# One score unit in sixty-four moved from ScalarE's exponential to a copy by VectorE and a power on GpSimd

## The chip, the cores and the metric

The kernel runs on one core of a Trainium2 chip. Its engines work side by side, each through its own instructions in order, and wait for each other by semaphores: TensorE (PE in the profile) multiplies matrices into eight PSUM banks, ScalarE (ACT) computes exponentials, VectorE (DVE) does elementwise work, copies and transpositions, GpSimd (POOL) so far only makes a few constants, and SyncE's queue (SP) starts transfers. The metric is the device time of one execution in microseconds.

## The reference

Two attentions over the same input `x` (2048 positions, width 640, 32 heads of 20) are mixed by a gate per position. The first is full softmax attention, the second a sliding one over 8 positions 2 apart.

```python
g = _sigmoid((x * gate_w).sum(-1, keepdims=True))
a = _A_ref(x, A_wqkv, A_wo)          # softmax(q k^T / sqrt(20)) v, all 2048 keys, then wo
b = _B_ref(x, B_wqkv, B_wo)          # the same over pos, pos-2, ..., pos-14
return g * a + (1 - g) * b
```

## The kernel before

Full attention is cut into 32 groups: 4 blocks of 512 queries (`qc`) times 8 quads of heads (`q`). A group has 64 units, 16 blocks of 128 keys (`kb`) times the 4 heads of the quad (`j`). For a unit, PE computes 128 keys by 512 queries of scores into one PSUM bank (L956), ACT takes the exponential into SBUF (`ebuf`, L969), and PE multiplies that by V and adds to the group's result in bank 5 (L977; V has a column of ones, so the sum of the exponentials comes with it). Units are taken in steps of three and two in turn, in banks 0 to 2 and 3 to 4; one ACT instruction serves a whole step. The scores of step s + 2 are issued right behind the exponential of step s. The four heads of a quad lie on different rows of the PE array for the scores and on different columns for the product.

At the end of a group `do_norm` transposes bank 5 into `rg` (L586) and `gen_norm` divides by the sums (L594, L595, L600) and transposes back into one of `NOT` = 16 slots of `oTn` (L603). The first product of the next group overwrites bank 5, so it waits for L586.

All other work is threaded between these steps by a planner written in Python, which keeps a clock for each engine, advanced by costs that are written at each operation. Work is cut into lanes (generators): `gen_k`, `gen_q` and `gen_v` project k, q and v for the coming groups; `gen_F` and `gen_K` make the sliding attention of a block of 512 positions, the former mainly projections and products, the latter mainly pairs of VectorE operations (L853 and L857, with L847 and L863 at the ends of a block of 128); `gen_fold` multiplies finished blocks with the output weights and stores them; `gen_prefold` does most of that for the last block, with copies at L653, and `last_fold` the rest (L665, L672) behind the loop. Lanes share PSUM banks 6 and 7: `take` claims one, `give` frees it when VectorE has copied it out. A lane has a first and a last step, counted by `gstep(g) = int(g * KBN * 4 / 2.5)`, 25.6 steps to a group, and is served when it is behind its share and the planner's clock has room. What has not been done when its result is needed is forced on the spot; what is left at the end of the loop is forced there, ahead of `last_fold`. The order that results is fixed: on the chip each engine runs its list as it stands.

The weights for a group's q projection are put in place by a VectorE copy within SBUF (L360); the projection (L378) waits for it. It is copied out at L537, made absolute at L538, corrected by a matmul at L543 that subtracts a bound of the scores, and copied to `qT` at L545.

Of the kernel before, what the change touches and what calls it, by code (L numbers as in the profile page):

```python
# [5 lines left out]
FP32 = mybir.dt.float32  # L6
# [212 lines left out]
def _build(ctx, nc, A_x, A_wqkv, A_wo, B_wqkv, B_wo, gate_w, out):  # L219
# [48 lines left out]
    qabs = sb([P, 512], BF16, "qabs")  # L268
    NEB = 3
    ebuf = [sb([P, 1536], BF16, "ebuf%d" % i) for i in range(NEB)]  # L270
    rg = [sb([P, 512], FP32, "rg%d" % i) for i in range(2)]
    rr = [sb([P, 16], FP32, "rr%d" % i) for i in range(2)]
    rgn = [sb([P, 16, 32], BF16, "rgn%d" % i) for i in range(2)]
    NOT = 16
    oTn = sb([P, NOT, 512], BF16, "oTn")
    itmp = oTn[:, 13, 0:256].bitcast(I32)
    stmp = oTn[:, 14, 0:320].bitcast(I32).rearrange("p (c k) -> p c k", c=CN)
    stmpf = oTn[:, 15, 0:320].bitcast(FP32).rearrange("p (c k) -> p c k", c=CN)
    zg = sb([P, KBN], FP32, "zg")
    gA = sb([P, 4 * KBN], FP32, "gA")  # L280
    gB = sb([P, KBN], FP32, "gB")
# [21 lines left out]
    def fap(t, first, dims):  # L303
        return bass.AP(tensor=t, offset=first.offset, ap=[[first.ap[0][0], P]] + dims)
# [30 lines left out]

    T("pe", pe_warm, reads=["ident", ("rgn", 0)], writes=[("bk", 7)])
    T("dve", lambda e: e.memset(e0[:, :], 0.0), writes=["e0"])
    T("dve", lambda e: e.memset(nsel[:, :], 0.0), writes=["nsel"])
    for j in range(4):
        T("dve", lambda e, j=j: e.memset(e0[32 * j:32 * j + 1, :], 1.0), writes=["e0"])  # L340
# [84 lines left out]
    def give(b, evac):  # L425
        held[b] = False
        if cur[0] is not None:
            cur[0].hold -= 1
        free_at[b] = evac.fin + 80.0
# [92 lines left out]
    def gen_q(gi):  # L522
        qc, q = divmod(gi, NQUAD)
        i = gi % 2
        yield ("dve", 370.0, 0.0)
        yield after(mk_wq(q, i))
        while qc == 0 and not kl[q].done:
            yield ("poll",)
        b = yield from take()
        yield from chain(b, proj_mms(b, WqP[i], qc), [("WqP", i), "xT"])  # L530
        yield ("dve", 690.0, 0.0)
        yield after(q_abs(b))
        yield ("pe", MM, 1.0)
        give(b, q_fin(b, gi, q))

    def q_abs(b):
        T("dve", lambda e: e.tensor_copy(qtmp[:, :], bank[b]), reads=[("bk", b)], writes=["qtmp"], cost=690)  # L537
        return T("dve", lambda e: e.tensor_scalar(qabs[:, :].bitcast(I16), qtmp[:, :].bitcast(I16), 0x7FFF, None,  # L538
                                                  op0=ALU.bitwise_and),
                 reads=["qtmp"], writes=["qabs"], cost=300)  # L540

    def q_fin(b, gi, q):
        T("pe", lambda e: e.matmul(bank[b], KM[:, q, :], qabs[:, :], start=False, stop=True, skip_group_check=True),  # L543
          reads=["qabs", ("KM", q)], accum=[("bk", b)], cost=MM)
        return T("dve", lambda e: e.tensor_copy(qT[gi % NQT][:, :], bank[b]), reads=[("bk", b)],  # L545
                 writes=[("qT", gi % NQT)], cost=690)

# [36 lines left out]
    def do_norm(gi):  # L584
        i = gi % 2
        return T("dve", lambda e: e.transpose(rg[i][:, :], bank[OB]), reads=[("ob", j) for j in range(4)],  # L586
                 writes=[("rg", i)], cost=720)

    def gen_norm(gi):
        qc, q = divmod(gi, NQUAD)  # L590
        i = gi % 2
        sl = gi % NOT
        yield ("dve", 420.0, 0.0)
        T("dve", lambda e: e.reciprocal(rr[i][:, :], rg[i][:, 0:512:32]), reads=[("rg", i)], writes=[("rr", i)], cost=240)  # L594
        T("dve", lambda e: e.tensor_tensor(rr[i][:, :], rr[i][:, :], gA[:, 16 * qc:16 * qc + 16], ALU.mult),  # L595
          reads=["gA"], writes=[("rr", i)], cost=180)
        rg_v = fap(rg[i], rg[i][:, 1:2], [[32, 16], [1, DH]])
        rr_b = fap(rr[i], rr[i][:, 0:1], [[1, 16], [0, DH]])
        yield ("dve", 500.0, 0.0)
        T("dve", lambda e: e.tensor_tensor(rgn[i][:, :, 1:1 + DH], rg_v, rr_b, ALU.mult),  # L600
          reads=[("rg", i), ("rr", i)], writes=[("rgn", i)], cost=500)
        yield ("dve", 710.0, 0.0)
        T("dve", lambda e: e.transpose(oTn[:, sl, :], rgn[i][:, :, :]), reads=[("rgn", i)], writes=[("oTn", sl)], cost=710)  # L603
        normdone[gi] = True
# [330 lines left out]
    free_at[6] = free_at[7] = t_  # L935


    units = [(qc, q, kb, j) for qc in range(QCN) for q in range(NQUAD) for kb in range(KBN) for j in range(4)]
    steps = []
    u = 0  # L940
    while u < len(units):
# [24 lines left out]
    def mk_exp(s):  # L966
        b0 = ST[s % 2][0]
        n = len(steps[s])
        return T("act", lambda e: e.activation(ebuf[s % NEB][:, 0:512 * n], ps[:, b0 * 512:(b0 + n) * 512], ACTF.Exp, scale=SCALE),  # L969
                 reads=[("bk", b0 + i) for i in range(n)], writes=[("ebuf", s % NEB)], cost=ED[n])  # L970

    def mk_pv(s, us):

        def fn(e):
            ins = None
            for i, (qc, q, kb, j) in us:
                ins = e.matmul(bank[OB][32 * j:32 * j + DH + 1, :], vA[:, q, kb, VW * j:VW * j + DH + 1],  # L977
                               ebuf[s % NEB][:, i * 512:(i + 1) * 512], start=(kb == 0), stop=(kb == KBN - 1))
            return ins

        rd = {("ebuf", s % NEB)}
        wr, ac = [], []
        for i, (qc, q, kb, j) in us:
            rd.add(("vA", q, kb // 3))
            (wr if kb == 0 else ac).append(("ob", j))
        T("pe", fn, reads=sorted(rd, key=str), writes=wr, accum=ac, cost=320)
# [6 lines left out]
    def lane(gen, name, s0, s1, total, pos=None):  # L993
        g = _Lane(gen, name, s0, s1, total)
        if pos is None:
            lanes.append(g)
        else:
            lanes.insert(pos, g)
        return g
# [59 lines left out]
        return int(g * KBN * 4 / 2.5)  # L1059

    kl, vl, ql, foldl = {}, {}, {}, {}
    vl[0] = lane(gen_v(0, 2), "v0", 0, 18, 10)
    lane(gen_late(), "late", 22, gstep(3), 1)
    FWIN = ((1.0, 8.3), (8.3, 13.2), (13.3, 18.3), (18.4, 23.5))
# [14 lines left out]
    for s in range(NS):  # L1079
# [4 lines left out]
        if first:  # L1084
            ng = gi + 1
            if ng < QCN * NQUAD:
                nqc, nq_ = divmod(ng, NQUAD)
                g_end = gstep(gi + 1)
                if nqc == 0:
                    kl[nq_] = lane(gen_k(nq_), "k%d" % nq_, s, g_end - 7, 20.0, 0)  # L1090
                    if nq_ % 2 == 1 and nq_ < NQUAD - 1:
                        p = (nq_ + 1) // 2
                        vl[p] = lane(gen_v(p), "v%d" % p, s + 2, gstep(gi + 2) - 2, 16.0)
                    ql[ng] = lane(gen_q(ng), "q%d" % ng, s + 4, g_end - 4, 6.0, 1)
                else:
                    ql[ng] = lane(gen_q(ng), "q%d" % ng, s + 2, g_end - 5, 6.0, 0)
        E = mk_exp(s)
        if s + 2 < NS:
            nxt = steps[s + 2]
# [8 lines left out]
            mk_qk(s + 2)  # L1108
        n1 = len(steps[s + 1]) if s + 1 < NS else 1
        lim = E.fin + ED[n1]  # L1110
        near = s + 1 < NS and (steps[s + 1][-1][2], steps[s + 1][-1][3]) == (KBN - 1, 3) or (
            s + 1 < NS and steps[s + 1][0][0:2] != steps[s + 1][-1][0:2])
        lim_pe = lim + 250.0
        lim_dve = lim + (0.0 if near else 450.0)
# [2 lines left out]
        def flush(must):  # L1117
            while pend:
                s0, i0, un0 = pend[0]
                g0 = un0[0:2]  # L1120
                obk = sch.bufs[("ob", 0)]
                if un0[2] == 0 and not must and obk[1]:
                    if max(t.fin for t in obk[1]) > clk["pe"] + 100.0:
                        return
                part = []
                while pend and pend[0][0] == s0 and pend[0][2][0:2] == g0:
                    _, i1, un1 = pend.pop(0)
                    part.append((i1, un1))
                for (_, un1) in part:
                    key = (un1[1], un1[2] // 3)  # L1130
                    if key not in vdone:
                        late.append((s, "v") + key)
                        force(vl[un1[1] // 2], s, lambda key=key: key in vdone)
                mk_pv(s0, part)
                if part[-1][1][2] == KBN - 1 and part[-1][1][3] == 3:
                    g1 = g0[0] * NQUAD + g0[1]
                    if g1 == 0 and not vl[0].done:
                        late.append((s, "gate", 0))
                        force(vl[0], s)
                    if g1 >= NOT and not folddone.get((g1 - NOT) // NQUAD):  # L1140
                        fl = foldl[(g1 - NOT) // NQUAD]
                        late.append((s, "fold", fl.name))
                        force(fl, s)
                    do_norm(g1)
                    lane(gen_norm(g1), "norm%d" % g1, s, s + 1, 1.0, 0)
# [63 lines left out]
```

## Time and profile before

| what | us |
|---|---|
| median of 2 runs | 1102.41 (1098.44 and 1106.39) |
| span of the profiled execution, first to last instruction | 1091.2 |
| exponentials, 819 instructions, busy | 956.0 |
| scores L956 and products L977, busy | 372.9 and 373.8 |
| VectorE busy | 579.7 |
| GpSimd busy | 0.7 |
| first exponential, start | 27.8 |
| last transposition of bank 5 (L586), start | 1081.0 |

The profile gives no time of its own for the profiled execution besides its span; the median of the runs is 11.2 us above it, which holds what lies ahead of the first instruction and behind the last. A row of the profile names the line, the engine, the operation, the tile written and the tile read with their shapes, then how often, the busy time and the mean of one in ns, and the idle time of the engine just before with what ended it. The groups are 29.2 to 35.5 us apart, from one L586 to the next.

### The profile page before, as it was taken

To read this page: it belongs to the slowest core of one execution; us is meant where nothing else is said; L and a number is where in the kernel's file an instruction comes from. 1 tells how busy PE (TensorE), PEld (TensorE's weight loads), DVE (VectorE), ACT (ScalarE), POOL (GpSimd) and SP (SyncE) were. 2 spreads that over 40 slices of the span, in tenths; PEclk is the share of its full clock that TensorE was granted. 3 is DMA by queue.
4 is the path that set the end of the run, shared out by engine and by line. 5 is a ranking of instruction groups with operands and counts; after the bars stand their busy time and mean duration, and the time that the engine had idled before them with its cause. 6 is when DMAs were issued, how large, how long until landed. Compare 5 with 4: busy or idle time off the path is not lost.

```text
span 1091.2 us, 15504 instructions
## 1 busy us (share of the span) xinstructions
PE 969.2 (89%) x5820; PEld 289.7 (27%) x5894; DVE 579.7 (53%) x1055; ACT 971.4 (89%) x842; POOL 0.7 (0%) x6
## 2 busy tenths in 40 slices
PE   6978899998798898989998988998888899799997
PEld 3323333322222222123332122233222223222231
DVE  4355434443635755762467767225787723777512
ACT  4868889988999988989999989999998989898996
POOL 0000000000000000000000000000000000000000
PEclk9879989998999756689998677999976699755695
DMA  8000000000000000000000000000000000000000
GB/s 277 1 1 15 17 1 2 1 23 9 1 2 1 1 1 1 1 1 7 7 7 7 1 1 1 7 8 7 7 2 1 1 7 13 7 1 1 1 1 25
DMA packets 11356, 12.79 MB, mean 12 GB/s; under 512 B 2708, under 2 KB 10644, under 8 KB 11284
## 3 DMA queue, kind: packets, MB, share of 16 engines
q1 hardware_dynamic: 9028, 11.27, 3.2%
q8 instruction: 49, 0.80, 0.3%
q10 hardware_dynamic: 2256, 0.53, 0.2%
q14 instruction: 23, 0.19, 0.1%
HBM read 9.18 MB, written 2.62 MB: 11 GB/s over the span
## 4 chain that ended last, share of the span: by engine, by line
PE 63%; ACT 21%; issue 9%; DVE 6%; DMA 1%; ACTq 0%; SPq 0%; DVEq 0%
ACT ebuf L969 21%; PE ps L956 20%; PE ps L378 19%; PE ps L977 19%; PE ps L453 2%; PE ps L543 1%; DVE bw L853 1%; PE ps L722 1%; DMA x_tm<-in_A_x_dram 1%; DVE blkacc L857 1%; PE ps L823 1%; DVE rg L586 1%; DVE qT L545 1%; DVE qtmp L537 0%; DVE WvB L672 0%
## 5 line engine op out<-in xcount | busy, mean ns | idle before, releaser
L969 ACT ACTIVATE ebuf<-ps 128x1536 bf16<-128x1536 f32 (+1 forms) x819 | 956.0, 1245 | 84.9 <-PE ps L956 64.3
L956 PE MATMUL ps<-qT,kT 32*128 32x512 bf16 x2048 | 372.9, 448 | 87.7 <-ACT ebuf L969 69.8
L977 PE MATMUL ps<-ebuf,vA 128*21 128x512 bf16 x2048 | 373.8, 452 | 3.3 <-DVE rg L586 1.2
L956 PEld LDWEIGHTS ps<-qT,kT 32*128 32x128 bf16 x2048 | 87.3, 93 | 370.5 <-PE ps L956 153.2
L977 PEld LDWEIGHTS ps<-ebuf,vA 128*21 128x21 bf16 x2048 | 77.7, 90 | 239.3 <-issue 229.7
L853 DVE TENSOR_TENSOR bw<-vB,bw 128x640 f32<-128x640 bf16 x112 | 91.9, 820 | 2.2
L857 DVE TENSOR_TENSOR blkacc<-blkacc,bw 128x640 f32<-128x640 f32 x96 | 79.0, 823 | 2.8
L739 DVE TENSOR_TENSOR prod<-qk 128x512 bf16<-128x512 bf16 x160 | 57.7, 418 | 22.3 <-PE ps L722 22.1
L707 DVE CAST qk<-ps 128x512 bf16<-128x512 f32 x40 | 27.6, 689 | 75.3 <-PE ps L378 72.6
L378 PE MATMUL ps<-xT,WqkB 128*128 128x512 bf16 x181 | 63.0, 413 | 3.2 <-issue 1.8
L537 DVE CAST qtmp<-ps 128x512 bf16<-128x512 f32 x32 | 22.1, 691 | 76.3 <-PE ps L378 73.6
L586 DVE STREAM_TRANSPOSE rg<-ps 128x512 f32<-128x512 f32 x32 | 22.9, 716 | 69.2 <-PE ps L977 69.2
L378 PE MATMUL ps<-xT,WqP 128*128 128x512 bf16 x134 | 52.1, 457 | 4.0 <-issue 1.8
L378 PE MATMUL ps<-woA_r,oTn 128*128 128x320 bf16 x240 | 54.2, 303 | 0.1
L390 DVE TENSOR_SCALAR kT<-ps,e 128x512 bf16<-128x512 f32 x28 | 20.9, 746 | 61.8 <-PE ps L378 60.0
L378 PE MATMUL ps<-xT,WkP 128*128 128x512 bf16 x145 | 48.8, 407 | 2.1 <-issue 1.0
L378 PE MATMUL ps<-WvA,oBacc 128*128 128x320 bf16 x160 | 38.0, 310 | 0.9 <-issue 0.4
L771 DVE CAST vB<-ps 128x512 bf16<-128x512 f32 x20 | 13.7, 687 | 46.5 <-PE ps L378 42.6
L633 DVE CAST outsb<-ps 128x320 bf16<-128x320 f32 x24 | 11.7, 488 | 44.7 <-PE ps L378 44.5
L545 DVE CAST qT<-ps 128x512 bf16<-128x512 f32 x32 | 22.1, 692 | 23.8 <-PE ps L543 22.6
L453 PE MATMUL ps<-WvA,xT 128*128 128x160 bf16 (+1 forms) x320 | 32.6, 244 | 1.5 <-DVE WvA L919 1.0
L378 PE MATMUL ps<-xT,WvB 128*128 128x512 bf16 x88 | 28.8, 389 | 0.8 <-DVE vB L771 0.4
(90 smaller groups left out, 448.4 us busy)
## 6 DMA issues: line engine op xcount, KB each, us to landing
x_tm<-in_A_x_dram SPq DMA_DIRECT2D x4, 640.0 KB
out_dram<-outsb SPq DMA_DIRECT2D x12, 160.0 KB
WqkB<-in_B_wqkv_dram SPq DMA_DIRECT2D x1, 1600.0 KB
WqkA<-in_A_wqkv_dram SPq DMA_DIRECT2D x2, 700.0 KB
WvA<-in_A_wqkv_dram SPq DMA_DIRECT2D x1, 800.0 KB
qk<-in_B_wqkv_dram SPq DMA_DIRECT2D x1, 800.0 KB
woA_r<-in_A_wo_dram SPq DMA_DIRECT2D x32, 25.0 KB
WvA<-in_B_wo_dram SPq DMA_DIRECT2D x5, 160.0 KB
```

What stands on the lines that cost most here:

```text
L378: ins = e.matmul(o, l, r, start=(k0 + k == 0), stop=(k0 + k == n - 1))
L453: ins = e.matmul(bank[b][:, i_ * wn:(i_ + 1) * wn], xT[:, c, kb * P:(kb + 1) * P], WvA[:, c, w0:w0 + wn], start=(c == 0), stop=(c == CN - 1))
L537: T("dve", lambda e: e.tensor_copy(qtmp[:, :], bank[b]), reads=[("bk", b)], writes=["qtmp"], cost=690)
L545: return T("dve", lambda e: e.tensor_copy(qT[gi % NQT][:, :], bank[b]), reads=[("bk", b)], writes=[("qT", gi % NQT)], cost=690)
L586: return T("dve", lambda e: e.transpose(rg[i][:, :], bank[OB]), reads=[("ob", j) for j in range(4)], writes=[("rg", i)], cost=720)
L707: give(b, T("dve", lambda e, dst=dst, b=b: e.tensor_copy(dst, bank[b]), reads=[("bk", b)], writes=[key], cost=690))
L739: t = T("dve", lambda e, r=r, f=f, off=off: e.tensor_tensor(prod[r][:, :], qB[:, f, :], kB[:, f, off:off + 512], ALU.mult), reads=["qB", " ...
L853: T("dve", lambda e, vv=vv, av=av: e.tensor_tensor(tmpB, vv, av, ALU.mult), reads=[("aT", ai), "vB4"], writes=["tmpB"], cost=822)
L857: T("dve", lambda e: e.tensor_tensor(blkacc[:, :, :], blkacc[:, :, :], tmpB, ALU.add), reads=["tmpB"], writes=["blkacc"], cost=822)
L956: ins = e.matmul(bank[b0 + i], kT[32 * j:32 * j + 32, q, kb * P:(kb + 1) * P], qT[gi % NQT][32 * j:32 * j + 32, :], start=True, stop=True)
L969: return T("act", lambda e: e.activation(ebuf[s % NEB][:, 0:512 * n], ps[:, b0 * 512:(b0 + n) * 512], ACTF.Exp, scale=SCALE), reads=[("bk" ...
L977: ins = e.matmul(bank[OB][32 * j:32 * j + DH + 1, :], vA[:, q, kb, VW * j:VW * j + DH + 1], ebuf[s % NEB][:, i * 512:(i + 1) * 512], start ...
```

## The change

The unit (`kb` = 15, `j` = 3) of each group leaves the steps, which then run over 63 units a group. A new lane `gen_x`, started at the group's first step and placed ahead of the others, claims bank 6 or 7, computes the unit's scores there, has VectorE copy them to SBUF as float32 (`px`), and GpSimd raise e^(1/sqrt(20)), a constant broadcast along the row, to that power into `xo` in bfloat16. `x_pv` puts the product of `xo` with V ahead of the group's other late products: from key block 10 on when the planner's clock says that the power is done, at the latest behind the last unit of key block 14. The last product of a group is now that of (15, 2), and the product of head 3 no longer ends its sum at key block 15 but at 14. To make room in SBUF, the two buffers `rg` become one and `NOT` goes from 16 to 15. `gstep` stays as it was.

```diff
-    rg = [sb([P, 512], FP32, "rg%d" % i) for i in range(2)]
+    rg1 = sb([P, 512], FP32, "rg")
+    rg = [rg1, rg1]
+    px = sb([P, 512], FP32, "px")
+    xo = sb([P, 512], BF16, "xo")
+    ebase = sb([P, 1], FP32, "ebase")
...
-    NOT = 16
+    NOT = 15
...
+    T("dve", lambda e: e.memset(ebase[:, :], float(np.exp(SCALE))), writes=["ebase"])
...
-    units = [(qc, q, kb, j) for qc in range(QCN) for q in range(NQUAD) for kb in range(KBN) for j in range(4)]
+    XU = (KBN - 1, 3)
+    units = [(qc, q, kb, j) for qc in range(QCN) for q in range(NQUAD) for kb in range(KBN) for j in range(4) if (kb, j) != XU]
+    xstate = {}
+    ebase_b = fap(ebase, ebase[:, 0:1], [[0, 512]])
+
+    def gen_x(gi):
+        qc, q = divmod(gi, NQUAD)
+        kb, j = XU
+        while ("qT", gi) not in qmade:
+            yield ("poll",)
+        b = yield from take()
+        yield ("pe", 330.0, 1.0)
+        T("pe", lambda e: e.matmul(bank[b], kT[32 * j:32 * j + 32, q, kb * P:(kb + 1) * P], qT[gi % NQT][32 * j:32 * j + 32, :],
+                                   start=True, stop=True),
+          reads=[("kT", q, kb // 4), ("qT", gi % NQT)], writes=[("bk", b)], cost=330)
+        yield ("dve", 690.0, 1.0)
+        give(b, T("dve", lambda e: e.tensor_copy(px[:, :], bank[b]), reads=[("bk", b)], writes=["px"], cost=690))
+        xstate[gi] = T("pool", lambda e: e.tensor_tensor(xo[:, :], ebase_b, px[:, :], ALU.pow), reads=["px", "ebase"], writes=["xo"],
+                       cost=9000.0)
+
+    def x_pv(gi):
+        qc, q = divmod(gi, NQUAD)
+        kb, j = XU
+        T("pe", lambda e: e.matmul(bank[OB][32 * j:32 * j + DH + 1, :], vA[:, q, kb, VW * j:VW * j + DH + 1], xo[:, :],
+                                   start=False, stop=False),
+          reads=["xo", ("vA", q, kb // 3)], accum=[("ob", j)], cost=320)
...
+            xl[gi] = lane(gen_x(gi), "x%d" % gi, s, s + 6, 2.0, 0)
...
+                if gx not in xdone and un0[2] >= 10:
+                    last = (KBN - 2, 3) in [x[2][2:4] for x in pend if x[0] == s0]
+                    if last and gx not in xstate:
+                        late.append((s, "x", gx))
+                        force(xl[gx], s)
+                    if gx in xstate and (last or xstate[gx].fin < clk["pe"] + 100.0):
...
+                        x_pv(gx)
+                        xdone.add(gx)
```

## The prediction

> **What bounds the kernel now.** I read the page from its first part to its fourth, then the groups of instructions with shapes kept apart, then the timeline of a few stretches.
>
> ```profile
> span 1091.2 us, 15504 instructions
> PE 969.2 (89%) x5820; PEld 289.7 (27%) x5894; DVE 579.7 (53%) x1055; ACT 971.4 (89%) x842; POOL 0.7 (0%) x6
> ...
> DVE  4355434443635755762467767225787723777512
> ACT  4868889988999988989999989999998989898996
> ...
> PEclk9879989998999756689998677999976699755695
> ```
>
> PE and ACT are both near full, VectorE (DVE) is half idle, GpSimd (POOL) does nothing. The granted TensorE clock swings between full and half; its mean is 0.831.
>
> ```profile
> L969 ACT ACTIVATE ebuf<-ps 128x1536 bf16<-128x1536 f32 x410 | 597.8, 1458 | 63.7 <-PE ps L956 55.7 <-PE ps L977 1.5
> L969 ACT ACTIVATE ebuf<-ps 128x1024 bf16<-128x1024 f32 x409 | 421.5, 1031 | 21.2 <-PE ps L977 11.6 <-PE ps L956 8.6 <-ACT ebuf L969 0.3
> ```
>
> Those are the exponentials, three or two units an instruction. Their idle is 63.7 + 21.2 = 85 us, so ACT is the bound for most of the time and PE for the rest. The timeline says where. At half clock without other matmuls:
>
> ```profile
> 409.10 0.61 PE L956 MATMUL ps<-qT,kT 32*128 32x512 bf16 x3
> 409.64 0.61 PE L977 MATMUL ps<-ebuf,vA 128*21 128x512 bf16 x3
> 410.18 0.60 PE L956 MATMUL ps<-qT,kT 32*128 32x512 bf16 x2
> 410.72 0.60 PE L977 MATMUL ps<-ebuf,vA 128*21 128x512 bf16 x2
> 411.41 0.61 PE L956 MATMUL ps<-qT,kT 32*128 32x512 bf16 x3
> ```
>
> A batch of scores (L956) or of products with V (L977) takes 0.54 us from start to start, two units or three alike. Four make 2.16 us, and the next round starts after 2.31 (411.41 - 409.10): ACT sets that, 0.462 us a unit. One more matmul of 0.54 us from the side work makes PE the later one. At full clock a batch takes 0.32 us (428.25 to 428.57), a round 1.28, so ACT sets the pace and side matmuls are hidden. If the mean clock mixes halves and wholes, half clock holds about (1 - 0.831) x 2 = 34% of the span.
>
> **The ACT side.** 32 of 2048 units leave ACT. The listed order has 806 exponentials instead of 819, so the change does what it says. Where ACT is the bound this gives 32 x 0.462 = 14.8 us; over 66% of the time, -9.8 us.
>
> **The PE side.** The unit that leaves needs a score matmul and a product of its own. A group had 25.6 rounds' batches of each kind; it has 25.2 and two more: 50.4 + 2 against 51.2, +1.2 batches. At full clock ACT hides them. At half clock they cost 1.2 x 0.54 x 32 x 34% = +7 us. ACT and PE together: -3 us. That is what the idea is worth.
>
> **The VectorE side.** Each group adds one copy out of PSUM, like the 691 ns casts at L537: 32 x 0.69 = 22 us on an engine that is 53% busy. One result buffer in place of two for the transposed outputs, and 15 slots in place of 16, bind only if a group's norm is a whole group late; the groups are 33 us apart and the norm takes 2.5. More q projections are forced just ahead of their use (6 for 3) and one fold; ACT has two exponentials queued over each, some 2.3 us, against 0.69 + 0.29 + 0.69 of VectorE work with a matmul between. I take nothing for these, +6 us in the range.
>
> **The tail.** This is in the order and not in the diff. The lanes' due steps still count 25.6 steps to a group, and there are now 25.2. With the added copies and matmuls in the plan the side work slides: the plan no longer finishes it inside the loop. The 88 matmuls that prepare the last output block (8 chunks of 11; copied out at L653) now stand behind the last product with V, and 15 two-input operations of the sliding window's last block (L847 to L863) behind the last transposed output on VectorE. Before, VectorE had this there:
>
> ```profile
> 1059.84 0.49 DVE L653 COPY WqkB<-ps 128x320 f32<-128x320 f32 x1 [3.32 <-PE ps L378]
> 1080.96 0.72 DVE L586 STREAM_TRANSPOSE rg<-ps 128x512 f32<-128x512 f32 x1 [20.63 <-PE ps L977]
> ...
> 1082.74 0.71 DVE L603 STREAM_TRANSPOSE oTn<-rgn 128x512 bf16<-128x512 bf16 x1
> 1083.96 4.66 DVE L672 TENSOR_TENSOR WvB<-ps,WqkB 128x320 bf16<-128x320 f32 x8 [0.51 <-PE ps L665]
> ```
>
> The last chunk had been copied 21 us before the last transposition; only 10.2 us (1091.2 - 1080.96) follow. In the new order: transposition and norm 2.5, then 15 x (0.82 + 0.04) = 12.9, so the first two chunks, long computed, are copied from 15.4 us on. Six chunks follow in two banks, 11 matmuls each at the rates of the 16 matmuls at L665 (8 in 1.37 us and 8 in 2.32, that is 0.17 to 0.29): 11 to 19 us, to 26 to 34 us. Then 0.5 for a copy, 1.4 to 2.3 for the last 8 matmuls, and 7.7 (1091.2 - 1083.51) less the 0.5 of overlap: 36 to 44 us where there were 10. Against it, the group of those 88 matmuls took 33.1 us between transpositions and the one after it, free of them, 29.2: -4. Net +22 to +30; I take +26.
>
> **GpSimd's power.** No row shows it. Below, the two iotas of the start:
>
> ```profile
> 0.82 0.23 POOL L322 IOTA oTn<- 128x128 int32 x1 [0.38 <-POOLq L1194]
> 1.01 0.27 POOL L323 IOTA oTn<- 128x160 int32 x1
> ```
>
> 32 elements more cost 0.038 us, so 512 would take 0.7. Above, the plan's own figure in the diff, 9 us; its figures for VectorE agree with the rows (690 for 691 ns, 720 for 716, 822 for 820, 1880 for 1882), so I take 9. The product that reads the result stands 12 to 16 score batches behind the unit's own, at 1.28 us an exponential (1052 us over 819) 15 to 20 us; 9 + 1.1 of matmul and copy fit. A page would have it shorter: the Trainium skill, GPSIMD Engine Reference, section 3.1, has a two-input GpSimd operation at about 2.6 cycles an element at 1.2 GHz, an estimate of 1.1 us for 512, and by it the next cost vanishes and the sum is 1125.
>
> **Does VectorE stand still meanwhile?** The trace has no stretch with both at work, so the cost lies between nothing and the power's whole length. I count what the order makes of it. From 1.1 to 10.1 us after its score matmul the power runs. If VectorE's next operation with two inputs in SBUF must wait, all behind it waits: the norm, the copy that forms the next q weights (L360), the emptying of banks 6 and 7; PE stops, in order, at its first matmul that needs one of them, and ACT runs dry two exponentials later. In 14 groups that matmul comes 2 batches after the unit's own (2.6 us: 7.5 us lost), in five others 3 to 5 (4.7 lost): 105 + 24 = +129 us. If copies and one-input operations within SBUF wait too, and the first of them always loses, 20 groups lose 7.5 and nine 3.7: 183. If GpSimd starts so late that four such operations pass first, PE's need comes 9 batches or more later in nearly all groups and nothing is lost. I take 129: the power waits for that one copy, its queue is empty, and a reciprocal of 0.25 us mostly stands between. A rule of the Trainium skill speaks here, against the change: SBUF — State Buffer, section Who interferes with whom, says GpSimd and VectorE share one pair of ports under an exclusive lock, that a VectorE instruction with two SBUF inputs contends with a GpSimd instruction that reads SBUF, and that the loser "fully blocks". No run here shows it yet; by it the sum is the one with the hold.
>
> **Rivals, with their times.** All start from the median, 1102.4; the profile's span is 11.2 us shorter, launch and end, which I carry over.
>
> 1. VectorE is held: 1102.4 - 3 + 26 + 129 = 1254; 1217 to 1335 with a hold between 90 and 183 and, as PE idles, more of the half clock. For it: the short distances above, VectorE at seven tenths in the late slices, no slack on ACT to win time back. Against it: nothing but that no row shows it. Six in ten.
> 2. No hold, the tail pays: 1102.4 - 3 + 26 = 1125, 1115 to 1140. For it: the order, which is certain. 22 in 100.
> 3. The other side, not slower: ACT's relief is had in full. If PE has its clock throughout, the two extra batches hide, ACT gives 14.8, and the tail runs at the fast rate, +22, less another 4 each for two more groups that lose late side work as the one above: 1102.4 - 14.8 + 14 = 1102, 1085 to 1115. It decides where half clock falls under 10% of the span; the clock row speaks against it. One in ten.
> 4. The power is longer than its place: above about 17 us each further us is waited for at the unit's product, 32 us in all; with 20 us and a hold the total passes 1335. For it: the 9 us are only the plan's. 8 in 100.
>
> **How the numbers follow.** I predict rival 1's time with a little for the half clock, 1260. The range runs from 1115 to 1335: it leaves out 3 and 4, 18 in 100. Case 1's own range is 1217 to 1335. Two per cent, about what a measurement of this kernel can tell from none, is 1124.5: cases 1 and 4 are above it and a little over half of 2, so slower 0.80, same 0.18. Faster by 2% would take 22 us, more than the relief of 14.8: 0.02.
>
> **What would show it.** The power's row on POOL: its mean says 9 us or not. Held: the two-input rows (rr L595, rgn L600, L853) or the copy of L360 with durations of several us or unexplained idle ahead of them during each power, PE waiting for DVE some 4 us a group, ACT's idle up from 85 to over 200. Not held: those rows as before, PE waiting on POOL nowhere. The tail: the last transposition of the outputs some 36 to 44 us before the end instead of 10. Wrong altogether if that distance stays near 10, or if the power waits for VectorE instead and only its own product is late.

## The result, and the profile after

The changed kernel takes 3232.6 us (3232.1 and 3233.1) against 1102.4: a ratio of 2.93 (95% interval 2.916 to 2.951). The forecast was 1260 us, within 1115 to 1335. The direction was right, the size was not nearly.

The page of the kernel after: its busy times, two rows of its slices, and the chain of work that ended last, by engine:

```profile
span 3231.3 us, 15622 instructions
PE 1065.5 (33%) x5821; PEld 303.3 (9%) x5894; DVE 615.1 (19%) x1088; ACT 963.7 (30%) x830; POOL 2622.6 (81%) x38
...
POOL 5878766898877988877968888976789888789884
PEclk7665666565665555565665555566655555656656
...
POOL 79%; PE 14%; POOLq 3%; DVE 2%; ACT 1%; issue 1%; DMA 0%; DVEq 0%; another core or an unknown queue 0%; SPq 0%; ACTq 0%
```

GpSimd, idle before, is now busy for 81% of the span and holds 79% of the chain that ended last. The other engines do about what they did before, in three times the span. In the changed kernel's line numbers, L958, L962, L963 and L969 are the unit's scores, copy, power and product; L989, L1002 and L1010 are the scores, exponentials and products of the steps; L594 is the transposition of bank 5 and L661 the copies of L653. The groups of instructions of the same page (busy, mean in ns, then idle ahead and what ended it):

```profile
L963 POOL TENSOR_TENSOR xo<-ebase,px 128x512 bf16<-128x512 f32 x32 | 2621.9, 81934 | 563.0 <-DVE px L962 348.4
...
L969 PE MATMUL ps<-xo,vA 128*21 128x512 bf16 x32 | 19.2, 600 | 2043.8 <-POOL xo L963 2043.8
...
L861 DVE TENSOR_TENSOR bw<-vB,bw 128x640 f32<-128x640 bf16 x112 | 92.0, 821 | 2.5
...
L865 DVE TENSOR_TENSOR blkacc<-blkacc,bw 128x640 f32<-128x640 f32 x96 | 79.1, 824 | 3.0
```

One power takes 81.9 us, not 9. PE reaches the unit's product (L969) and waits for it 2044 us in all, 63.9 each, so the product stands 81.9 - 63.9 = 18 us behind the power's start. The power starts 1.3 to 2.2 us behind the unit's scores, so that is some 20 us behind those, at the upper end of the 15 to 20 us that the prediction counted. VectorE's two-input operations keep their durations (L861 and L865 are L853 and L857 of before, 820 and 823 ns), though 164 of these 208 now run beside a power. The timeline of PE shows one such wait, of a power that started at 849.57:

```profile
866.62 0.39 PE L989 MATMUL ps<-qT,kT 32*128 32x512 bf16 x3
931.83 0.60 PE L969 MATMUL ps<-xo,vA 128*21 128x512 bf16 x1 [64.81 <-POOL xo L963]
931.83 1.02 PE L1010 MATMUL ps<-ebuf,vA 128*21 128x512 bf16 x3
```

The end of the kernel after, on VectorE, answers to the end of before shown in the prediction:

```profile
3196.52 0.72 DVE L594 STREAM_TRANSPOSE rg<-ps 128x512 f32<-128x512 f32 x1 [0.76 <-PE ps L1010]
...
3198.93 0.78 DVE L855 TENSOR_TENSOR blkacc<-vB,bw 128x640 f32<-128x640 bf16 x1
...
3210.79 0.82 DVE L871 TENSOR_TENSOR oBacc<-blkacc,bw 128x640 bf16<-128x640 f32 x1
3211.53 1.01 DVE L661 COPY WqkB<-ps 128x320 f32<-128x320 f32 x2
...
3222.69 0.49 DVE L661 COPY WqkB<-ps 128x320 f32<-128x320 f32 x1 [1.00 <-PE ps L383]
3224.07 4.66 DVE L680 TENSOR_TENSOR WvB<-ps,WqkB 128x320 bf16<-128x320 f32 x8 [0.89 <-PE ps L673]
```

From the last transposition to the end are 34.8 us (3231.3 - 3196.5) in place of 10.2: the tail is there, step for step. It is 25 us of an excess of 2130 (3232.6 - 1102.4).

### The profile page after: what moved, and what is told of

It is laid out like the page before. It is cut to its first block, busy times and chain, and to the rows that moved or that the text cites. A ratio compares the mean times of both kernels' runs of the same rounds, so it can differ in the third digit from the quotient of the medians.

```text
span 3231.3 us, 15622 instructions
## 1 busy us (share of the span) xinstructions
PE 1065.5 (33%) x5821; PEld 303.3 (9%) x5894; DVE 615.1 (19%) x1088; ACT 963.7 (30%) x830; POOL 2622.6 (81%) x38
## 4 chain that ended last, share of the span: by engine, by line
POOL 79%; PE 14%; POOLq 3%; DVE 2%; ACT 1%; issue 1%; DMA 0%; DVEq 0%; another core or an unknown queue 0%; SPq 0%; ACTq 0%
POOL xo L963 79%; PE ps L989 4%; PE ps L1010 4%; PE ps L383 4%; POOLq L146 3%; ACT ebuf L1002 1%; DVE px L962 1%; PE ps L969 1%; PE ps L458 0%; PE ps L958 0%; PE ps L730 0%; PE ps L831 0%; DMA x_tm<-in_A_x_dram 0%; DVE rg L594 0%; DVE bw L861 0%
## 5 line engine op out<-in xcount | busy, mean ns | idle before, releaser
L963 POOL TENSOR_TENSOR xo<-ebase,px 128x512 bf16<-128x512 f32 x32 | 2621.9, 81934 | 563.0 <-DVE px L962 348.4
L1002 ACT ACTIVATE ebuf<-ps 128x1536 bf16<-128x1536 f32 (+2 forms) x807 | 948.5, 1241 | 2206.9 <-PE ps L989 2191.2
L969 PE MATMUL ps<-xo,vA 128*21 128x512 bf16 x32 | 19.2, 600 | 2043.8 <-POOL xo L963 2043.8
L989 PE MATMUL ps<-qT,kT 32*128 32x512 bf16 x2016 | 397.5, 485 | 71.7 <-ACT ebuf L1002 49.6
L1010 PE MATMUL ps<-ebuf,vA 128*21 128x512 bf16 x2016 | 405.1, 491 | 2.0 <-DVE rg L594 2.0
L969 PEld LDWEIGHTS ps<-xo,vA 128*21 128x21 bf16 x32 | 3.0, 93 | 2055.9 <-POOL xo L963 2055.9
L989 PEld LDWEIGHTS ps<-qT,kT 32*128 32x128 bf16 x2016 | 85.9, 95 | 381.0 <-PE ps L989 161.4
L747 DVE TENSOR_TENSOR prod<-qk 128x512 bf16<-128x512 bf16 x160 | 58.3, 422 | 282.1 <-PE ps L730 281.8
L1010 PEld LDWEIGHTS ps<-ebuf,vA 128*21 128x21 bf16 x2016 | 78.0, 91 | 258.0 <-issue 246.4
L861 DVE TENSOR_TENSOR bw<-vB,bw 128x640 f32<-128x640 bf16 x112 | 92.0, 821 | 2.5
L594 DVE STREAM_TRANSPOSE rg<-ps 128x512 f32<-128x512 f32 x32 | 22.9, 716 | 309.1 <-PE ps L1010 307.8
L865 DVE TENSOR_TENSOR blkacc<-blkacc,bw 128x640 f32<-128x640 f32 x96 | 79.1, 824 | 3.0
L838 DVE COPY bw<-ps 128x1024 bf16<-128x1024 bf16 x16 | 10.9, 684 | 264.9 <-PE ps L831 264.9
```

The costliest lines, as they stand in the source:

```text
L747: t = T("dve", lambda e, r=r, f=f, off=off: e.tensor_tensor(prod[r][:, :], qB[:, f, :], kB[:, f, off:off + 512], ALU.mult), reads=["qB", " ...
L861: T("dve", lambda e, vv=vv, av=av: e.tensor_tensor(tmpB, vv, av, ALU.mult), reads=[("aT", ai), "vB4"], writes=["tmpB"], cost=822)
L865: T("dve", lambda e: e.tensor_tensor(blkacc[:, :, :], blkacc[:, :, :], tmpB, ALU.add), reads=["tmpB"], writes=["blkacc"], cost=822)
L963: xstate[gi] = T("pool", lambda e: e.tensor_tensor(xo[:, :], ebase_b, px[:, :], ALU.pow), reads=["px", "ebase"], writes=["xo"], cost=9000.0)
L969: T("pe", lambda e: e.matmul(bank[OB][32 * j:32 * j + DH + 1, :], vA[:, q, kb, VW * j:VW * j + DH + 1], xo[:, :], start=False, stop=False) ...
L989: ins = e.matmul(bank[b0 + i], kT[32 * j:32 * j + 32, q, kb * P:(kb + 1) * P], qT[gi % NQT][32 * j:32 * j + 32, :], start=True, stop=True)
```

## Is it the power's own length?

Theory A: the power costs by column, and its length is the whole excess. Rivals: VectorE is held while GpSimd works (B), the new lane costs by itself (C), most of the 81.9 us is fixed (D). The ratios below are against runs of the kernel before in the same round as the variant, whose medians were 1098 to 1107 us. The "blind sum" of the expected texts is the sum of the prediction.

**e1: a multiplication in place of the power.**

```diff
-        ... e.tensor_tensor(xo[:, :], ebase_b, px[:, :], ALU.pow) ...
+        ... e.tensor_tensor(xo[:, :], ebase_b, px[:, :], ALU.mult) ...
```

> The power becomes a multiplication of the same tiles on GpSimd, so one unit in 64 has no exponential and the output is another. Everything else, order included, is that of the change. Theory A (the power's own 81.9 us are the whole excess): GpSimd's instruction falls to about 1 to 2 us, PE's wait for GpSimd at the unit's product from 2044 us to near 0, and the time is what the blind sum has without a hold: 1102 - 3 + 26 = 1125 us, within 1105 to 1140. Rival B (VectorE stands still while GpSimd works): the same here up to 32 x 1.5 = 48 us more. Rival C (the new lane and its place in PE's order cost by themselves, whatever GpSimd does): well above 1150, with PE still waiting at the product.

Measured: 1138.9 us, ratio 1.038 (1.032 to 1.045), near the upper end of what theory A expected. GpSimd's row and that of the unit's product:

```profile
L963 POOL TENSOR_TENSOR xo<-ebase,px 128x512 bf16<-128x512 f32 x32 | 33.8, 1057 | 1035.5 <-DVE px L962 569.7 <-DVE rr L602 465.8
...
L969 PE MATMUL ps<-xo,vA 128*21 128x512 bf16 x32 | 15.4, 480 | 0.5 <-DVE zg L485 0.5
```

GpSimd's operation takes 1.06 us, with the same broadcast constant and the same tiles, and PE's wait at the product is gone; C falls. One word of the code is worth 3232.6 - 1138.9 = 2094 us; PE's wait of 2044 us is nearly all of it. The remaining 36 to 39 us over before are what the rest of the change costs: 26.1 of them in the tail (36.3 us from the last transposition to the end), the rest in the loop.

**e2 and e8: the power of 56 and of 256 columns.**

```diff
-        ... e.tensor_tensor(xo[:, :], ebase_b, px[:, :], ALU.pow) ...
+        ... e.tensor_tensor(xo[:, 0:NX], ebase_b, px[:, 0:NX], ALU.pow) ...
```

> The power is taken of 56 of the 512 columns; the other 456 columns of the unit's exponentials stay zero, so the output is another. Theory A with a cost by column (81.9 / 512 = 0.160 us): the power takes 9.0 us, which is the length that the plan assumed, it fits into the 15 to 20 us to its product, and the time is that of e1 within 1%. Rival D (most of the 81.9 us is a fixed cost, code loading or a start): the power stays above 40 us and the time above 1900. Rival B (VectorE's two-input operations stand still for the whole power, which the prediction took as likeliest): e1 plus 90 to 183 us, and rows L603, L608 or L861 of several us.

> The power over 256 columns, the rest of the unit's exponentials zero, in the order of the change. Theory A: a straight line through 56 columns (9.28 us) and 512 (81.93 us) gives 41.1 us for the power; the wait of PE at the product is what exceeds the 15 to 20 us of its place, and with the 17 us that the change has between two powers the groups come every 58 us: 28 + 32 x 58 + 36 = about 1920 us and a launch of 5 to 11. Rival D (a jump between 56 and 512 columns): anything else than 38 to 44 us.

GpSimd's rows, first of e2, then of e8 (the edit adds lines, so the power is L965 here, and what is L603 in the kernel after is L604):

```profile
L965 POOL TENSOR_TENSOR xo<-ebase,px 128x56 bf16<-128x56 f32 x32 | 297.0, 9281 | 765.6 <-DVE px L964 436.7 <-DVE rr L603 328.8
```

```profile
L965 POOL TENSOR_TENSOR xo<-ebase,px 128x256 bf16<-128x256 f32 x32 | 1316.3, 41134 | 561.6 <-DVE px L964 349.6 <-DVE rr L603 212.0
```

9.28, 41.13 and 81.93 us for 56, 256 and 512 columns are a straight line of 0.159 us a column and 0.36 us to start; D falls. e2, with a power as long as the plan assumed, takes 1127.2 us (ratio 1.027, 1.021 to 1.032), and PE waits 0.5 us in all at the product, so a power of 9 us is hidden and the likeliest case of the prediction, a hold worth 129 us, does not exist. The time is 1.0% under that of e1, at the edge of what was expected. e8 takes 1925.0 us against the expected 1920 and a launch. From e8 to the whole power the time grows by 1308 us for 40.8 us more of power, 32 for one: above its place of 18 us each further microsecond of the power is paid 32 times.

**How long is VectorE held?** The prediction asked for L603 (its L595) with durations of several us. Before, that row was

```profile
L595 DVE TENSOR_TENSOR rr<-rr,gA 128x16 f32<-128x16 f32 x32 | 5.6, 174 | 1.1
```

In 15 of 32 groups it now comes right behind the power's start. The timelines of the kernel after, of e8, of e2 and of e1 at such a place:

```profile
949.19 81.92 POOL L963 TENSOR_TENSOR xo<-ebase,px 128x512 bf16<-128x512 f32 x1 [17.42 <-DVE rr L602]
949.21 1.05 DVE L603 TENSOR_TENSOR rr<-rr,gA 128x16 f32<-128x16 f32 x1
950.29 0.50 DVE L608 TENSOR_TENSOR rgn<-rg,rr 128x320 bf16<-128x320 f32 x1
```

```profile
469.69 41.12 POOL L965 TENSOR_TENSOR xo<-ebase,px 128x256 bf16<-128x256 f32 x1 [16.10 <-DVE rr L603]
469.72 0.62 DVE L604 TENSOR_TENSOR rr<-rr,gA 128x16 f32<-128x16 f32 x1
```

```profile
281.97 9.26 POOL L965 TENSOR_TENSOR xo<-ebase,px 128x56 bf16<-128x56 f32 x1 [26.55 <-DVE rr L603]
282.00 0.28 DVE L604 TENSOR_TENSOR rr<-rr,gA 128x16 f32<-128x16 f32 x1
```

```profile
905.33 1.04 POOL L963 TENSOR_TENSOR xo<-ebase,px 128x512 bf16<-128x512 f32 x1 [29.37 <-DVE rr L602]
905.35 1.04 DVE L603 TENSOR_TENSOR rr<-rr,gA 128x16 f32<-128x16 f32 x1
```

VectorE is held: 1.05 - 0.17 = 0.87 us behind 512 columns, 0.44 behind 256, 0.11 behind 56. In e1 the row takes 1.04 us as well, behind an operation of 1.04 us. So the hold goes with the columns that GpSimd reads, some 1.7 ns each ((0.87 - 0.11) / 456), and not with how long it computes; at 950.29 the next two-input operation runs at its usual 0.50 us with 80 us of the power still to come.

In two groups it is GpSimd that loses. There an operation of VectorE with two inputs (L747) stands at the power's start:

```profile
849.57 82.20 POOL L963 TENSOR_TENSOR xo<-ebase,px 128x512 bf16<-128x512 f32 x1 [16.00 <-DVE px L962]
849.58 0.42 DVE L747 TENSOR_TENSOR prod<-qk 128x512 bf16<-128x512 bf16 x1
```

L747 keeps its usual 0.42 us, and the power takes 0.28 us more than the 81.92 of the other thirty. In e1, e2 and e8 GpSimd's operation is as much longer in the same two groups.

So B is real and worth an estimated 32 x 0.9 = 29 us of VectorE's time at most. What it costs the kernel is not shown: e1 and e2 have the same order and differ in the hold (0.87 and 0.11 us), and e1 is 12 us slower, but the runs of either lie 10 to 13 us apart.

## What the rest of the change costs, and the tail

**e3: the due steps counted by 63 units.**

```diff
-        return int(g * KBN * 4 / 2.5)
+        return int(g * (KBN * 4 - 1) / 2.5)
```

> e1 with the due steps counted by 63 units a group instead of 64. Theory T (the late due steps push the last block's side work behind the loop): the last transposition of the outputs stands 10 to 15 us before the end as before the change, and the time is 15 to 30 us under e1's, some 1095 to 1105. Rival (the added copy and matmuls alone push it out): the distance stays above 30 us and the time at e1's.

Measured: 1130.8 us, ratio 1.033 (1.025 to 1.041); the distance at the end stays 35.8 us. Theory T fell: the due steps are not what pushes the side work out of the loop, and the rival came.

**e5: the plan's own cost of an exponential, on top of e3. e6: the same edit alone on the kernel before.**

```diff
-    ED = {3: 1345.0, 2: 917.0, 1: 500.0}
+    ED = {3: 1400.0, 2: 960.0, 1: 500.0}
```

> e3 with one edit to the plan: its cost of an exponential goes from 1345 and 917 ns to 1400 and 960, so that its clock leaves as much room beside the exponentials as the chip does. In the order all side work is then inside the loop again. Theory T2 (the plan ran out of room, and the side work behind the loop costs the 26 us of the blind sum): the distance from the last transposition of bank 5 to the end falls from 36 to about 10 us, and the time from 1131 to 1100 to 1112 us. Rival (the side work costs the loop what it saves behind it): the distance falls, the time stays within 8 us of e3's.

> The control for e5: the kernel before with the same edit of the plan's cost. Its side work was already inside the loop, so theory T2 expects no change beyond 1% (1089 to 1111 us). Rival: the edit by itself makes a better order, and gives 1% or more here too.

In e5 the distance at the end is 10.1 us: the side work is inside the loop again, so the plan had run out of room. But the time rises to 1158.0 us (ratio 1.051, 1.043 to 1.059), which neither T2 nor its rival expected. Between the fourth and the fifth transposition of bank 5 now lie 63.4 us, where the other groups take 28 to 39: in this order v projections are forced there ahead of their use, and the exponentials stand still. Their row among the waits of e5 is

```profile
ACT ebuf L1002 <- PE ps L989: 132.8, 161, 25.8
```

that is 132.8 us in 161 waits, the longest of them 25.8 us. The run says nothing against T2 and does not show it. e6 takes 1107.3 us, ratio 1.006 (1.001 to 1.011): the edit by itself gains nothing.

**e10: wider limits for the side work, on top of e5. e11: both edits on the kernel before.**

```diff
-        lim_pe = lim + 250.0
-        lim_dve = lim + (0.0 if near else 450.0)
+        lim_pe = lim + 350.0
+        lim_dve = lim + (0.0 if near else 600.0)
```

> e5 with the same wider limits, so without the 63.4 us group. Theory T2 (the side work left behind the loop is what e3 and e1 lose): the tail is 10 us instead of 36 and the time 1131 - 26 = about 1105, at most 1115. Rival (the side work costs the loop what it saves behind it): within 8 us of e3's 1131.

> Control for both: the kernel before with the same plan costs and wider limits. Nothing was left behind its loop, so 1090 to 1110, within 1% of before; if it gains as much as e9 does, the gain of e9 is the plan's and not the unit's.

e10 takes 1092.3 us, ratio 0.988 (0.985 to 0.992), with no group over 37.3 us. Its last transposition stands 10.3 us before the end of its span of 1094.0 us:

```profile
1083.73 0.72 DVE L594 STREAM_TRANSPOSE rg<-ps 128x512 f32<-128x512 f32 x1 [21.97 <-PE ps L1010]
```

By the ratios e10 is 4.3% under e3, by the spans 31 us (1125.0 and 1094.0), of which 25.5 are the tail. What T2 expected came, and the loop did not pay for the side work: from the first exponential to the last transposition it has 1055.8 us, and 1061.1 in e3. The granted clock differs too (0.835 in e10's profile, 0.811 in e3's), so only the 25.5 us at the end are clear of it. Nor is e10's span under the 1091.2 us of before, at a like clock (0.831). e11 takes 1116.6 us, ratio 1.011 (1.005 to 1.016), above the expected 1090 to 1110: the same edits make the kernel before no faster.

## Is the idea worth anything on another engine?

**e4, e7, e9: VectorE makes the unit's exponential.** One operation reads the scores in PSUM and writes their scaled value as a 16-bit integer that is the bit pattern of the exponential; the copy and GpSimd's part are gone. e4 has it in e3's plan, e7 with the edit of e5 and 16 slots, e9 with the limits of e10 as well.

```diff
-        give(b, T("dve", lambda e: e.tensor_copy(px[:, :], bank[b]), ...))
-        xstate[gi] = T("pool", lambda e: e.tensor_tensor(xo[:, :], ebase_b, px[:, :], ALU.pow), ...)
+    XA, XB = 128.0 * SCALE / float(np.log(2.0)), 128.0 * 127.0 - 7.4
+        xstate[gi] = T("dve", lambda e: e.tensor_scalar(xo[:, :].bitcast(I16), bank[b], XA, XB, op0=ALU.mult, op1=ALU.add), ...)
+        give(b, xstate[gi])
```

> GpSimd and the copy are left out: VectorE makes the unit's exponential itself, straight from PSUM, in one operation that writes scaled scores as the 16-bit pattern of a bfloat16 (a piecewise linear exponential, off by up to some 3%, for one unit in 64), due steps counted by 63. Theory A: as fast as e3, since VectorE has the same number of operations of the same 0.69 us: 1090 to 1105 us, that is 0 to 1% under the kernel before, never 15 us under it, because the ACT relief is bounded by 14.8 us. Rival (PE's two extra batches a group take the relief back): within 0.5% of before or over it.

> e4 (VectorE makes the unit's exponential as a bit pattern) with the edit of e5 and the 16th slot of the outputs back, which spares the fold that is forced at group 15. Tail back to 10 us from 36, groups 14 and 15 at about 33 us instead of 37: 1114 - 26 - 8 = 1080 us, at the best side of what the ACT relief of 14.8 us allows, 1.5% under before. Rival (the relief is spent on the two extra batches a group and PE sets the time): 1090 to 1105, the same as before.

> e7 with a plan that leaves nothing to be forced but one early q projection: the limits up to which side work may run past an exponential go from 250 and 450 ns to 350 and 600. e7 lost some 30 us in one group (63.4 us, forced v projections) of its 1127. Theory: that stall goes, the tail stays at 10 us, and the time is 1128.6 - 30 = about 1098, between 1085 and 1105, no better than before by 2%, as ACT's relief is bounded by 14.8 us and PE's extra batches take part of it. Rival (the unit on VectorE is worth its full relief): 1075 to 1085.

e4 takes 1114.5 us, ratio 1.015 (1.011 to 1.019), with 35.6 us at its end: over the expected 1090 to 1105, and slower than before by less than its tail. e7 takes 1128.6 us, ratio 1.025 (1.018 to 1.031), also over both of its expectations: the tail is 10.0 us, but one group takes 63.4 us as in e5. The two groups at the forced fold (14 and 15 in the expectation) take 34.4 and 32.8 us in place of 37.8 and 37.1, as expected of the 16th slot; e5, with the same plan costs and 15 slots, has 38.9 and 36.7. e9 has neither loss:

```profile
span 1077.5 us, 15515 instructions
PE 967.9 (90%) x5823; PEld 290.5 (27%) x5894; DVE 596.4 (55%) x1088; ACT 956.8 (89%) x830; POOL 0.7 (0%) x6
```

1075.4 us, ratio 0.974 (0.969 to 0.979): 2.6% faster than before, and the version to keep if an exponential that is off by up to some 3% in one unit of 64 is allowed (worked out from the line's two constants; no run measures it). Expected were 1098, or 1075 to 1085 by the rival, which came. The gain of 23 to 34 us is above the 14.8 that ACT's relief can give; the control e11 has the same edits of the plan and is slower, so they alone are not it either. The record points at the clock for the rest: in this round e9 ran at a granted clock of 0.831 to 0.848 and before at 0.814 to 0.832. Where both have 0.831, in the two profiles, e9's span is 13.7 us under that of before (1077.5 and 1091.2) and its loop 15.0 (1038.2 and 1053.2), about the relief alone. That is one execution of each, and why e9 is granted the higher clock stays open.

**e12: a second unit of each group.** `XUS = [(KBN - 1, 2), (KBN - 1, 3)]`, two operations and one batch of two products.

> e9 with a second unit of each group, (15, 2), made by VectorE in the same way, due steps counted by 62, and plan costs and limits (1460 and 1000 ns, 450 ns) at which nothing is forced early. Theory (ACT is the bound and VectorE has room): another 32 x 0.46 us = 15 us of exponentials leave ACT, the two products of a group go side by side, so PE gets about as many batches as in e9; the time is 1075 - 5 to 15 = 1060 to 1070. Rival (PE and its half clock are the bound now): 1070 to 1085, no change from e9. Rival (VectorE at seven tenths in the late groups): over 1085.

1093.9 us, ratio 0.996 (0.993 to 0.999): over the 1060 to 1070 of the theory, and in the range of the last rival. The second unit gives nothing on top of the first; as the plan's settings differ from e9's too, the run does not tell whether PE, VectorE or the order takes it back.

## Why the prediction was wrong

- The step that failed is "I take 9". The plan's figure for the power was taken over because the plan's figures for VectorE agree with their rows. For the power there was no row to agree with; it takes 81.9 us, and 9 us are enough for 56 of its 512 columns. With 81.9 us in its place the prediction's own rule, "each further us is waited for at the unit's product, 32 us in all", and the 18 us measured for its "about 17" give 32 x (81.9 - 18) = 2045 us, which is the wait measured. The fourth rival was the case that came, with 8 in 100, and its price reached only a little past 1335, as no bound above 9 us was set.
- The hold: its direction and place were right, its length was not. It was taken as the whole power; it is 0.87 us. The rule of the Trainium skill (SBUF — State Buffer, section Who interferes with whom), that one pair of ports is locked and the loser "fully blocks", is seen here at the power's start. By the Trainium skill (SBUF — State Buffer, section SBUF: two separate sides) the first has the pair "for the whole instruction"; that is not seen, as the hold ended 0.87 us into 81.9. By the Trainium skill's GPSIMD Engine Reference, section 2.1, a two-input body takes at most one operand a cycle, at 1.2 GHz by its section 1: an estimate of 0.85 us for 2 x 512, beside the 0.87 measured.
- The estimate from section 3.1 of the Trainium skill's GPSIMD Engine Reference, 1.1 us for 512 columns, fits the multiplication of e1 (1.06 us) and not the power, which is 77 times that. The section's figure is for an addition.
- The tail, +26 us: +24.6 in the kernel after, +26.1 in e1. The step was right, though two misses in it cancel in part: the stretch at the end was put at 36 to 44 us and took 34.8 to 36.3, and of the 4 us that the loop was to win back there, the group that took 33.1 shows 0.5 in e1 (32.6) and 3 in e2 (30.1). The sum without a hold, 1125, was near as well: e2, whose power is hidden, took 1127.2. Of the two reasons given for the tail the due steps fell (e3); the added work that the plan had no room for stands (e5, e10).
- ACT and PE, -3 us: in the loops, from the first exponential to the last transposition, e2 has 1055.2 us and e1 1070.3 against 1053.2 before, so 2 to 17 us were lost instead, at a lower granted clock (0.810 and 0.799 against 0.831). What lowers it is not shown. The exponentials are 807, not 806. The forced fold was priced at nothing with 6 us in the range: in e4 the two groups at it lose some 8 to e7's.
- All sums start from the median and take the 11.2 us between it and the profile's span for launch and end. On record every run's time is 1.8 to 2.2 us above its span (here 3233.1 and 3231.3). The other 9 us are only that the profiled execution of before was a quicker one than the median: its runs lie between 1092 and 1112 us in all rounds.
- Slower at 0.80 came true, for a reason that held 8 of those 80. That is luck.

## What to carry to other kernels

A cost that a program writes beside an operation is a claim, and where no row of a trace shows that operation, its bound above is open, whatever the other figures do: measure the one instruction by itself before a plan is built on it. Compare its cost by column, too: 0.16 us a column, measured once on a few columns, would have shown that 512 of them take 82 us and can't fit a group of 33 us. And after a planner's input changes, look at what its fixed order leaves behind the loop.

## What the runs showed of the hardware

GpSimd's power of float32 values takes 0.159 us a column of 128 partitions and 0.36 us to start, the same for every group's data (81.92 us, and 82.20 in the two groups beside L747), against a mean of 1.06 us for a multiplication of the same 512 columns. A two-input operation of VectorE right behind GpSimd's start is held for some 1.7 ns for each column that GpSimd reads (two operands; 0.87 us for 512), equally for the power and the multiplication, and then runs freely beside it. With PE idle for two thirds of the time, the granted clock fell to a mean of 0.597, from 0.831.
